# A gated-attention and mixture-of-experts kernel: expert 0's rest in 64-row pairs, with turns on VectorE

## The chip, the cores and the metric

One Trainium2 chip; the kernel runs on one core of it. The metric is the device time of one execution in microseconds (us), the median of the runs. TensorE (PE) multiplies, VectorE (DVE), ScalarE (ACT) and GpSimd (POOL) work element by element, SyncE (SP) and POOL issue the DMAs.

## The reference

```python
# attention: q, k, v, o_gate (4, 8, 768, 40); a state C, n, m per batch and head
for t in range(S):
    m_new = np.maximum(f_gate[:, :, t] + m, i_gate[:, :, t])
    f_stab = np.exp(f_gate[:, :, t] + m - m_new)
    i_stab = np.exp(i_gate[:, :, t] - m_new)
    C = f_stab * C + i_stab * einsum('bhd,bhe->bhde', vt, kt)
    n = f_stab * n + i_stab * kt
    y[:, :, t] = sigmoid(o_gate) * (C @ qt) / max(abs(n . qt), 1)
x = y.transpose(0, 2, 1, 3).reshape(3072, 320)
# experts: w1 (8, 320, 1024), w2 (8, 1024, 320)
logits = x @ w_gate + log1p(exp(x @ w_noise)) * noise
top2, top2_w = the two largest of 8 and their softmax
for e in range(8):
    out[tokens of e] += weight * (np.maximum(x[tokens of e] @ w1[e], 0) @ w2[e])
```

## The kernel before

**Stages.** The attention runs in 24 units of 128 tokens. Its rows go to DRAM (`rows`), and the gate, the choice of two experts and each token's rank within its expert are worked out beside it, in steps of a generator (`g_part`) that VectorE does in between. After the attention the eight experts follow one another. For each, POOL gathers the token rows into `XG`, tile by tile (128 rows, 7 tiles at most); the rows are turned so that the 320 features lie on partitions; the first product (`mm1` or `mm1_rows`) gives `hx`, 1024 by tokens; ScalarE evicts its relu (`HH`), VectorE the low part (`HLO`); the second product (`mm2`) gives y for 128 tokens, VectorE scales it, and POOL adds it into the output rows by an indirect DMA (`put`). Every operand is split into a high and a low part and a product is three: high by high, low by high, high by low. ScalarE makes the high part, VectorE the low one.

**Experts 0 and 1** have their tokens in two pieces, the first 384 columns and a rest of 416 (`E0S`), since the first piece is known earlier. The order is: first piece of 0 (`mm1(0, 0, f)`, eight passes `f`), its outputs (`first_outputs(0)`), first piece of 1, its outputs, rest of 1 (`mm1(1, 1, f)`), its four tiles of outputs (`mm2(1, t)`, t = 3 to 6), rest of 0, its outputs, and then experts 2 to 7 whole. `first_outputs` holds three sums in PSUM and goes through them three times, 72 products; its `events` are steps of other work that are put between two products. One of them is `advance`, which counts a unit up, does a share of the routing on VectorE, and sends the products for ranks (`ranks`, lines 480 to 482) and for the one-hot bursts (line 491) to PE once their unit has come (`lag`).

**Turning.** Experts 0 and 1 turn their rows on PE (`transpose_x`, line 883), ScalarE and VectorE writing the halves `XH` and `XL` from PSUM. With three blocks of 128 features a pass of `mm1` has 8 products: 128 rows of weights twice and 64 rows once, the last with two parts side by side. Experts 2 to 7 turn on VectorE in blocks of 32 (`turn_x`, to `XB`), 16 DMAs bring the blocks to their places (`spread_x`, to `XT`), ScalarE and VectorE split them (`split_x`, to `XH5`, `XL5`), and `mm1_rows` takes five blocks of 64 features, two products at a time on the two halves of the array's rows, each half for other rows of `hx` (`j` and `j + 4`).

**Queues.** The code is written in the order in which each engine does its work. Each engine takes its instructions in order, so an instruction that waits holds all behind it on its engine; SP and POOL do so with the DMAs that they issue. The PSUM banks of the experts have names: `s0` and `s1` with two buffers each, `e`, `xt`, `st`, `o`. `bank("h")` goes round `s0`, `s1`, `e` for `mm1`, `bank("x")` gives those of the transposes, `bank("y")` those of `mm2`.

Of the kernel before, what the change touches and what calls it, by code (L numbers as in the profile page):

```python
# [51 lines left out]
TURNS2 = {3: (3, 4), 4: (5,), 5: (6,)}  # L52
REST = (3, 4, 5, 6)
SPLITS2 = (5, 0, 3, 2)
# [20 lines left out]
def build(ctx, tc, qk, vk, og, fi, noise, wgn, w1, w2, cst, ce, out):  # L75
# [980 lines left out]

    def split_x(e):
        QC, QO = quarters(e)
        for h in range(2):
            c = slice(QO[2 * h], QO[2 * h] + 2 * QC[2 * h])  # L1060
            fx = lambda a: a[:, c].rearrange("p (q t c) -> p q t c", q=2, c=32)
            fh = lambda a: a[:, c].rearrange("p (t q c) -> p q t c", q=2, c=32)
            for k in range(5):
                A.activation(fh(XH5[:, k]), fx(XT[:, k]), AF.Copy)  # L1064
                V.tensor_sub(fh(XL5[:, k]), fx(XT[:, k]), fh(XH5[:, k]).bitcast(F32))  # L1065
                yield
# [77 lines left out]
    def mm2(e, t, between={}, base=None):  # L1144
# [3 lines left out]
        if t < 6:  # L1148
            c = slice(128 * t, 128 * t + n)
            for j in range(8):  # L1150
                T.matmul(ps[0:n], HH[:, j, c], W2H[:, j], start=j == 0, stop=False)  # L1151
                T.matmul(ps[0:n], HH[:, j, c], W2L[:, j], start=False, stop=False)  # L1152
                T.matmul(ps[0:n], HLO[:, j, c], W2H[:, j], start=False, stop=j == 7)  # L1153
                if j in between:
                    between[j]()
        else:

            for j in range(8):
                T.matmul(ps[0:2 * n], HT[:, j, 0:2 * n], W2H[:, j], start=j == 0, stop=False)
                T.matmul(ps[0:2 * n], HT[:, j, 0:2 * n], W2L[:, j], start=False, stop=j == 7)  # L1160
            A.activation(y[0:n], ps[n:2 * n], AF.Copy)
            V.tensor_add(y[0:n], y[0:n], ps[0:n])
            ps = y
# [57 lines left out]
    side = split_w1(staged, V)  # L1221
    def first_outputs(e, events):
        sums = [bank("h")[:, 0:DM] for _ in range(3)]
# [40 lines left out]
    lag[:] = 14, 14  # L1264
    rest = iter(range(7 - 1, 8))
    turn_ = iter(range(3))
    for t, y in first_outputs(0, at((lambda: transpose_x(next(turn_)), (3, 8, 13)), (lambda: next(side), (18, 40, 48)),
# [6 lines left out]
    load_w1(0, RAW1)  # L1274
# [13 lines left out]
    turn_ = iter(REST)  # L1288
    for t, y in first_outputs(1, at((low_w2b, range(2, 34, 4)), (lambda: advance(0.3), range(1, 40, 2)),
                                    (lambda: transpose_x(next(turn_)), (46, 52, 58, 64)))):  # L1290
        put(1, t, y)
# [4 lines left out]
    turns = lambda *ts: {n: (lambda t=t: transpose_x(t)) for n, t in zip((2, 4, 6), ts)}  # L1296
    weigh(1, 1)
    load_w2(0)
    gather(0, 1)
    side = split_w1(RAW1, V)  # L1300
    for f in range(8):
        mm1(1, 1, f)
        next(dealing, None)
        if f > 3:
            next(side)
    run(dealing)
    gather(2, ts=(0, 1, 2))
    for n, t in enumerate(REST):
        y = mm2(1, t, turns(*((3, 4, 5), (6,), (), ())[n]))
        next(side, None)  # L1310
        put(1, t, y)
        if not n:
            weigh(0, 1)
        if n == 1:
            gather(2, ts=(3, 4))
        if n == 2:
            gather(2, ts=(5, 6))
        if n < 3:
            turn_x(2, n)
    rows_w1(2)  # L1320
    side = split_w2()
    for f in range(8):
        mm1(0, 1, f)
        next(side)
        for t in TURNS2.get(f, ()):
            turn_x(2, t)
        if f == max(TURNS2):
            spread_x(2)
            weigh(2)
# [9 lines left out]
    XH5 = m2.tile([128, 5, NT], FR, name="xh5")  # L1339
# [217 lines left out]
```

## Time and profile before

| | |
|---|---|
| runs | 505.16, 502.9, 505.0 us; median 505.0 |
| profiled execution | 501.79 us, of which the span is 500.0; mean granted clock 0.992 |
| PE busy | 482.9 us, 97% of the span, 5653 matmuls |
| VectorE, ScalarE, POOL busy | 331.7 (66%), 249.3 (50%), 230.9 (46%) |
| read and written in HBM | 53.51 and 17.28 MB, 142 GB/s over the span |

The profile is one execution; times in it count from the start of the span. A row of the timeline gives the start, the time in us, the engine, the line of the code, the operation with its tile, and in brackets how long the engine had been idle and what ended that. PE's starts are measured and its ends modelled, so two products overlap in the rows; PE's pace is read from one start to the next. In the table by stage the first number is the length of the stretch, and then each engine's busy time in it with its count of instructions. DMA times to landing count from the issue.

### The profile page before, as it was taken

The page shows a single profiled execution, that of the slowest core. Times are in us where ns is not written, and L with a number is a line of the kernel's source. Part 1 is how long each engine was busy: PE and PEld are TensorE (multiplying, and loading weights), DVE is VectorE, ACT ScalarE, POOL GpSimd, SP SyncE. Part 2 cuts the span into 40 slices and gives each one's busy share as a digit, 9 for nine tenths or more (in the row PEclk, how much of TensorE's full clock was granted, in tenths as well). Part 3 has the DMA queues.
Part 4 walks back from the last instruction along what each step waited for, and adds up shares of the span by engine and source line. Part 5 has one row for each costly group of instructions (what it writes and reads, how often), then busy time and mean ns, then how long its engine had stood idle before and what let it go on. Part 6 is the DMA issues. An engine that isn't in the chain of part 4 may idle for free.

```text
span 500.0 us, 14344 instructions
## 1 busy us (share of the span) xinstructions
PE 482.9 (97%) x5653; PEld 451.1 (90%) x5653; DVE 331.7 (66%) x899; ACT 249.3 (50%) x604; POOL 230.9 (46%) x302
## 2 busy tenths in 40 slices
PE   8899999998999999999999999999999999999995
PEld 4677778777998999999999999999999999999994
DVE  7888988987599657585774566285637548554410
ACT  7687887798645244354551444063424605513400
POOL 9656675275404374828138306801850480142043
PEclk9899998999999999999999999999999999999999
DMA  6899787887799562859579528926971891682032
GB/s 166 229 262 269 218 242 202 230 225 214 232 384 279 138 120 54 184 112 263 137 149 267 135 53 209 248 41 139 254 139 42 206 256 26 141 176 37 4 39 41
DMA packets 62025, 84.52 MB, mean 169 GB/s; under 512 B 10790, under 2 KB 50347, under 8 KB 61920
## 3 DMA queue, kind: packets, MB, share of 16 engines
q1 hardware_dynamic: 49584, 59.21, 44.5%
q0 software_dynamic: 12368, 24.33, 23.0%
q8 instruction: 46, 0.75, 0.6%
q14 instruction: 27, 0.22, 0.1%
HBM read 53.51 MB, written 17.28 MB: 142 GB/s over the span
## 4 chain that ended last, share of the span: by engine, by line
PE 85%; DVE 6%; POOL 2%; ACT 2%; DMA 2%; issue 2%; SPq 0%; POOLq 0%; ACTq 0%; DVEq 0%
PE s L1091 17%; PE e L1091 8%; PE s L1105 6%; PE o L1151 5%; PE o L1153 5%; PE o L1152 5%; PE st L1151 5%; PE st L1153 4%; PE st L1152 4%; PE o L404 3%; PE s L365 3%; PE e L1105 3%; PE st L394 2%; PE e L342 2%; PE xt L427 2%
## 5 line engine op out<-in xcount | busy, mean ns | idle before, releaser
L1177 POOL DMA_INDIRECT y_out<-y,tok x53 | 86.3, 1628 | 167.3 <-DVE y L1167 150.6
L1129 ACT ACTIVATE hx<-s 128x384 fp32r<-128x384 f32 (+3 forms) x85 | 39.3, 496 | 71.8 <-PE s L1091 57.0
L1132 DVE SCALAR_TENSOR_TENSOR hx<-s,hx 128x384 fp32r<-128x384 f32 (+1 forms) x85 | 44.8, 548 | 37.5 <-ACT hx L1129 37.2
L854 POOL DMA_INDIRECT xg<-rows,tok x53 | 57.7, 1088 | 22.3 <-issue 13.1
L1151 PE MATMUL o<-w2h,hx 128*128 128x320 f32 (+1 forms) x184 | 57.3, 311 | 0.0
L1153 PE MATMUL o<-w2h,hx 128*128 128x320 f32 (+1 forms) x184 | 56.7, 308 | 0.0
L1152 PE MATMUL o<-w2l,hx 128*128 128x320 f32 (+1 forms) x184 | 56.6, 308 | 0.0
L1151 PE MATMUL st<-w2h,hx 128*128 128x320 f32 x152 | 47.5, 312 | 0.0
L1153 PE MATMUL st<-w2h,hx 128*128 128x320 f32 x152 | 46.9, 308 | 0.0
L1152 PE MATMUL st<-w2l,hx 128*128 128x320 f32 x152 | 46.8, 308 | 0.0
L1064 ACT ACTIVATE xh<-xt__124 128x384 fp32r<-128x384 f32 (+1 forms) x60 | 27.1, 528 | 20.2 <-DMA xt__124<-xb 16.5
L416 POOL TENSOR_TENSOR raw<-tm,vk 128x320 f32<-128x320 f32 x24 | 21.1, 877 | 31.7 <-ACT vk L351 11.3
L351 ACT ACTIVATE vk<-vk 128x320 f32<-128x320 f32 x72 | 33.8, 469 | 2.8 <-DMA vk<-og_in 1.9
L1151 PEld LDWEIGHTS o<-w2h,hx 128*128 128x128 f32 (+1 forms) x184 | 34.4, 187 | 0.5 <-issue 0.5
L1152 PEld LDWEIGHTS o<-w2l,hx 128*128 128x128 f32 (+1 forms) x184 | 34.5, 187 | 0.0
L1153 PEld LDWEIGHTS o<-w2h,hx 128*128 128x128 f32 (+1 forms) x184 | 34.3, 187 | 0.0
L1091 PE MATMUL s<-xh,w1h 64*128 64x384 f32 (+3 forms) x320 | 34.1, 340 | 0.0
L1091 PE MATMUL s<-xl,w1h 64*128 64x384 f32 (+3 forms) x320 | 34.0, 338 | 0.0
L1091 PE MATMUL s<-xh,w1l 64*128 64x384 f32 (+3 forms) x320 | 33.7, 337 | 0.0
L365 PEld LDWEIGHTS s<-qk 64*64 64x64 f32 x768 | 26.0, 141 | 8.5 <-issue 6.5
L1167 DVE TENSOR_SCALAR y<-o,gw 128x320 f32<-128x320 f32 x22 | 12.1, 551 | 32.4 <-PE o L1153 32.4
L1065 DVE TENSOR_TENSOR xl<-xt__124,xh 128x384 fp32r<-128x384 f32 (+1 forms) x60 | 31.2, 568 | 2.7 <-ACT xh L1064 1.9
(321 smaller groups left out, 1327.0 us busy)
## 6 DMA issues: line engine op xcount, KB each, us to landing
raw<-w_in SPq DMA_DIRECT2D x14, 640.0 KB, 12.7
raw<-w_in SPq DMA_DIRECT2D x7, 1280.0 KB, 10.3
xt__124<-xb SPq DMA_DIRECT2D x72, 120.0 KB, 3.2
qk<-qk_in SPq DMA_DIRECT2D x24, 256.0 KB, 4.6
y_out<-zrow SPq DMA_DIRECT2D x15, 320.0 KB, 7.0
vk<-vk_in POOLq DMA_DIRECT2D x24, 162.0 KB, 4.7
vk<-vk_in SPq DMA_DIRECT2D x24, 162.0 KB, 5.4
vk<-og_in SPq DMA_DIRECT2D x24, 160.0 KB, 4.3
```

The costliest lines, as they stand in the source:

```text
L351: A.activation(g, g, (AF.Exp, AF.Ln, AF.Exp)[p], bias=float(p == 1), scale=(-1.0, 1.0, -1.0)[p])
L365: T.matmul(SQ[u][:, p][half[p], h, :], q[r, 1, h, :], q[r, 0, h, :], start=True, stop=True)
L854: P.indirect_dma_start(out=XG[0:rows_of(e, t), t], out_offset=None, in_=XD[0:n], in_offset=bass.IndirectOffsetOnAxis(ap=token(e, t), axis= ...
L1065: V.tensor_sub(fh(XL5[:, k]), fx(XT[:, k]), fh(XH5[:, k]).bitcast(F32))
L1091: T.matmul(ps[y][:, 0:n], a[r, k, s], x[r, k, c], start=i == 0, stop=i == len(ops) - 1)
L1105: T.matmul(ps[:, 0:n], l, r, start=i == 0, stop=i == len(ops) - 1)
L1129: A.activation(hi, x, AF.Relu)
L1132: V.scalar_tensor_tensor(lo, top[0], 0.0, top[1].bitcast(F32), op0=OP.max, op1=OP.subtract)
L1151: T.matmul(ps[0:n], HH[:, j, c], W2H[:, j], start=j == 0, stop=False)
L1152: T.matmul(ps[0:n], HH[:, j, c], W2L[:, j], start=False, stop=False)
L1153: T.matmul(ps[0:n], HLO[:, j, c], W2H[:, j], start=False, stop=j == 7)
L1177: apart(e, P.indirect_dma_start(out=out, out_offset=bass.IndirectOffsetOnAxis(ap=token(e, t), axis=0), in_=y[0:n], in_offset=None, **(how ...
```

## The change

It turns expert 0's rest on VectorE and multiplies it with `mm1_rows`, as experts 2 to 7. For that its gathers are issued one by one, each behind expert 1's transpose of the same tile of `XG` (`turn_and_gather`), ahead of the puts of expert 1's first outputs; the turns stand behind passes 1 and 2 of `mm1(1, 1, f)` (`TURNS0`); `spread_rest` brings 96 columns a quarter (128 in the first) to `XT` in 16 DMAs; `rows_w1(0)` loads the first weights in blocks of 64 rows; and `split_rows_w1` and `split_rest` stand between the tiles of `mm2(1, t)` (`SPLITS1`). `first_outputs` names its banks itself, its transposes too, and `lag` for the ranks is 18 in place of 14 there. `mm2` of expert 0 takes the column blocks in the order `JS`. `weigh(1, 1)` moves ahead of expert 1's transposes.

```diff
--- before.py
+++ after.py
@@ -49,8 +49,12 @@
 GATES = (6, 4, 4, 4, 4, 4, 4)
 LEAD = 2
 TURNS = {0: (0,), 1: (1,), 2: (2,), 3: (3,), 4: (4, 5), 5: (6,)}
-TURNS2 = {3: (3, 4), 4: (5,), 5: (6,)}
+TURNS0 = {1:(3,4),2:(5,6)}
+TURNS1 = {1:(0,1,2)}
+TURNS2 = {0: (3, 4), 1: (5, 6)}
 REST = (3, 4, 5, 6)
+JS = (0, 1, 2, 4, 5, 6, 3, 7)
+SPLITS1 = (3,2,0,5)
 SPLITS2 = (5, 0, 3, 2)
 SPLITS = (2, 2, 3, 3, 3, 2, 0)
 OR1 = (0, 6, 1, 2, 3, 4, 5)
@@ -1054,6 +1058,25 @@
             for m in range(4):
                 SP.dma_start(XT[32 * m:32 * m + 32, :, c], XB[r, 5 * (m % 2):5 * (m % 2) + 5, 0:QC[q]])
 
+    def spread_rest():
+        for q in range(4):
+            r = slice(32 * q, 32 * q + 32)
+            n = 96 if q else 128
+            for m in range(4):
+                SP.dma_start(XT[32 * m:32 * m + 32, :, 128 * q:128 * q + n], XB[r, 5 * (m % 2):5 * (m % 2) + 5, 96:96 + n])
+
+    def split_rest():
+        c, d = E0S[1], E0S[1] + 384
+        for k in range(5):
+            x = XT[:, k, 0:512].rearrange("p (q t c) -> p q t c", q=4, c=32)[:, :, 0:3]
+            to = lambda a: a[:, k, c:d].rearrange("p (t q c) -> p q t c", q=4, c=32)
+            A.activation(to(XH5), x, AF.Copy)
+            V.tensor_sub(to(XL5), x, to(XH5).bitcast(F32))
+            if k == 4:
+                A.activation(XH5[:, :, d:NS], XT[:, :, 96:128], AF.Copy)
+                V.tensor_sub(XL5[:, :, d:NS], XT[:, :, 96:128], XH5[:, :, d:NS].bitcast(F32))
+            yield
+
     def split_x(e):
         QC, QO = quarters(e)
         for h in range(2):
@@ -1141,18 +1164,16 @@
         else:
             later.append(rest)
 
-    def mm2(e, t, between={}, base=None):
+    def mm2(e, t, base=None):
         n = rows_of(e, t)
         ps = bank("y")[:, 0:DM]
         y = m2.tile([128, DM], F32, name="y", bufs=TA + 1)
         if t < 6:
             c = slice(128 * t, 128 * t + n)
-            for j in range(8):
+            for j in (JS if e == 0 else range(8)):
                 T.matmul(ps[0:n], HH[:, j, c], W2H[:, j], start=j == 0, stop=False)
                 T.matmul(ps[0:n], HH[:, j, c], W2L[:, j], start=False, stop=False)
                 T.matmul(ps[0:n], HLO[:, j, c], W2H[:, j], start=False, stop=j == 7)
-                if j in between:
-                    between[j]()
         else:
 
             for j in range(8):
@@ -1219,8 +1240,12 @@
 
     wipe = lambda: next(clear, None)
     side = split_w1(staged, V)
+    def open_bank(name):
+        return psum.tile([128, 512], F32, name=name, bufs=2 if name in ("s0", "s1") else 1)
+
     def first_outputs(e, events):
-        sums = [bank("h")[:, 0:DM] for _ in range(3)]
+        sums = [open_bank(name)[:, 0:DM] for name in (("s0","s1","s0"),("s0","s1","e"))[e]]
+        turn["h"] += 2
         for k, (l, r) in enumerate(((HH, W2H), (HLO, W2H), (HH, W2L))):
             for n in range(24):
                 t, j = divmod(n, 8)
@@ -1261,17 +1286,18 @@
             next(side)
         advance(0.7 if f < 4 else 0.3, 4, True)
     weigh(1, 0)
-    lag[:] = 14, 14
+    lag[:] = 18,14
     rest = iter(range(7 - 1, 8))
     turn_ = iter(range(3))
-    for t, y in first_outputs(0, at((lambda: transpose_x(next(turn_)), (3, 8, 13)), (lambda: next(side), (18, 40, 48)),
+    free = iter(("xt","st","s1"))
+    for t, y in first_outputs(0, at((lambda: transpose_x(next(turn_), open_bank(next(free))), (3, 8, 14)), (lambda: next(side), (18, 40, 48)),
                                     (lambda: low_w2(next(rest)), (2,6)),
                                     (wipe, range(1, 72, 2)), (lambda: advance(0.2), range(1, 36, 2)),
                                     (lambda: advance(0.3), range(37, 72, 2)))):
         held[t] = y
     for _ in clear:
         pass
-    load_w1(0, RAW1)
+    rows_w1(0)
     lag[:] = 6,4
     for f in range(8):
         mm1(1, 0, f, later)
@@ -1286,45 +1312,51 @@
         V.tensor_sub(W2L[:, x], RAW2[:, x], W2H[:, x].bitcast(F32))
 
     turn_ = iter(REST)
+
+    def turn_and_gather():
+        x = next(turn_)
+        transpose_x(x)
+        gather(0, ts=(x,))
+
     for t, y in first_outputs(1, at((low_w2b, range(2, 34, 4)), (lambda: advance(0.3), range(1, 40, 2)),
-                                    (lambda: transpose_x(next(turn_)), (46, 52, 58, 64)))):
-        put(1, t, y)
+                                    (lambda: weigh(1, 1), (44,)), (turn_and_gather, (46, 52, 58, 64)))):
+        held[t] = y
+    for t in range(3):
+        put(1, t, held[t])
     assert done[0] == NU
     while routing:
         fill(1.0)
     dealing = deal()
-    turns = lambda *ts: {n: (lambda t=t: transpose_x(t)) for n, t in zip((2, 4, 6), ts)}
-    weigh(1, 1)
     load_w2(0)
-    gather(0, 1)
-    side = split_w1(RAW1, V)
     for f in range(8):
         mm1(1, 1, f)
         next(dealing, None)
-        if f > 3:
-            next(side)
+        for t in TURNS0.get(f, ()):
+            turn_x(0, t)
+        if f == max(TURNS0):
+            spread_rest()
     run(dealing)
+    weigh(0, 1)
     gather(2, ts=(0, 1, 2))
+    XH5 = m2.tile([128, 5, NT], FR, name="xh5")
+    side = chain(split_rows_w1(), split_rest())
     for n, t in enumerate(REST):
-        y = mm2(1, t, turns(*((3, 4, 5), (6,), (), ())[n]))
-        next(side, None)
-        put(1, t, y)
-        if not n:
-            weigh(0, 1)
-        if n == 1:
-            gather(2, ts=(3, 4))
-        if n == 2:
-            gather(2, ts=(5, 6))
-        if n < 3:
-            turn_x(2, n)
+        for _ in range(SPLITS1[n]):
+            next(side, None)
+        put(1, t, mm2(1, t))
+        if n in (1, 2):
+            gather(2, ts=(2 * n + 1, 2 * n + 2))
+        for x in TURNS1.get(n, ()):
+            turn_x(2, x)
     rows_w1(2)
     side = split_w2()
-    for f in range(8):
-        mm1(0, 1, f)
+    for j in range(4):
+        mm1_rows(0, 1, j)
         next(side)
-        for t in TURNS2.get(f, ()):
+        next(side)
+        for t in TURNS2.get(j, ()):
             turn_x(2, t)
-        if f == max(TURNS2):
+        if j == max(TURNS2):
             spread_x(2)
             weigh(2)
     V.tensor_copy(toki, cs[:, C_TOK:C_TOK + NU])
@@ -1336,7 +1368,6 @@
     P.tensor_add(ov, ov, rf)
     P.tensor_scalar(ov, ov, float(BLK), None, op0=OP.is_ge)
     P.tensor_mul(OVM[:, :, 2:4], WTS[:, :, 0:2], ov)
-    XH5 = m2.tile([128, 5, NT], FR, name="xh5")
     side = chain(split_rows_w1(), split_x(2))
     for n, t in enumerate(REST):
         for _ in range(SPLITS2[n]):
```

PE, end of expert 0's first outputs (tile `e` or `s_2898` is the third sum; L480 to L482 are the ranks; L1105 or L1128 is the first pass of expert 1). Before:

```order
L1227 MATMUL s_2897<-w2l,hx 128x320 x8
L1227 MATMUL e<-w2l,hx 128x320 x2
L480 LDWEIGHTS tri
L480 MATMUL st<-xt__124,tri 128x64
L481 LDWEIGHTS ones
L481 MATMUL st<-xt__124,ones 128x64
L482 LDWEIGHTS ones
L482 MATMUL st<-xt__124,ones 128x8
L1227 MATMUL e<-w2l,hx 128x320 x6
L1105 MATMUL s_3063<-xl,w1h 128x384 x5
```

and of the change:

```order
L1252 MATMUL s_2897<-w2l,hx 128x320 x8
L1252 MATMUL s_2898<-w2l,hx 128x320 x8
L1128 MATMUL e<-xl,w1h 128x384 x5
L1128 MATMUL e<-xl,w1l 128x384 x3
L484 LDWEIGHTS tri
L484 MATMUL st<-xt__124,tri 128x64
L485 LDWEIGHTS ones
L485 MATMUL st<-xt__124,ones 128x64
L486 LDWEIGHTS ones
L486 MATMUL st<-xt__124,ones 128x8
L1128 MATMUL s_3070<-xl,w1h 128x384 x5
```

The ranks moved from the middle of the third sum to behind expert 1's first pass, and that pass begins on `e`.

VectorE, expert 1's four tiles of second products (`y<-o`, `y<-st` scale a tile; `xl` is the low part of x, `w1l` that of expert 0's first weights, `xb` a turn). Before:

```order
L886 TENSOR_TENSOR xl<-xt,xl 128x2x128
L887 TENSOR_TENSOR xl<-xt,xl 64x128
L1167 TENSOR_SCALAR y<-o,gw 128x320
L172 TENSOR_TENSOR w1l<-raw_119,w1h 128x512
L846 TENSOR_TENSOR gw_2710<-xg,km 128x8
L847 TENSOR_TENSOR gw<-gw_2710 128x4
L1048 STREAM_TRANSPOSE xb<-xg 128x5x2x32
L886 TENSOR_TENSOR xl<-s_3555,xl 128x2x32
L887 TENSOR_TENSOR xl<-s_3555,xl 64x32
L1167 TENSOR_SCALAR y<-st,gw 128x320
```

and of the change:

```order
L850 TENSOR_TENSOR gw_2710<-xg,km 128x8
L851 TENSOR_TENSOR gw<-gw_2710 128x4
L1099 TENSOR_TENSOR w1l<-raw_119,w1h 128x512 x3
L1188 TENSOR_SCALAR y<-o,gw 128x320
L1099 TENSOR_TENSOR w1l<-raw_119,w1h 128x512 x2
L1188 TENSOR_SCALAR y<-st,gw 128x320
L1052 STREAM_TRANSPOSE xb<-xg 128x5x2x32 x3
L1188 TENSOR_SCALAR y<-o,gw 128x320
L1074 TENSOR_TENSOR xl<-xt__124,xh_3502 128x4x3x32 x5
L1077 TENSOR_TENSOR xl<-xt__124,xh_3502 128x5x32
L1183 TENSOR_TENSOR y<-y,st 32x320
```

The low parts of x left the first tiles and stand behind the scaling of the third, tile 5.

SP, from expert 0's second weights (L832 or L836) to expert 2's first (L1071 or L1094). Before:

```order
L832 DMA raw_123<-w_in 128x8x320
L824 TENSOR_LOAD who
L1071 ISA
L1071 DMA raw_119<-w_in 64x5x512
L1071 ISA
L1071 DMA raw_119<-w_in 64x5x512
```

and of the change:

```order
L836 DMA raw_123<-w_in 128x8x320
L1066 DMA xt__124<-xb 32x5x128 x4
L1066 DMA xt__124<-xb 32x5x96 x12
L828 TENSOR_LOAD who
L1094 ISA
L1094 DMA raw_119<-w_in 64x5x512
```

Sixteen DMAs of the spread came in between.

## Rows read from the trace of the kernel before

**Rows 1.** Page, part 4: who held the chain that ended last, by engine
```profile
PE 85%; DVE 6%; POOL 2%; ACT 2%; DMA 2%; issue 2%; SPq 0%; POOLq 0%; ACTq 0%; DVEq 0%
```

**Rows 2.** Table by stage: core 0; columns us, PE, PEld, DVE, ACT, POOL busy, PEclk, DMA share, GB/s
```profile
140.40:154.34 13.94, 12.63 (x93) 11.88 (x93) 13.49 (x60) 5.55 (x14) 0.50 (x2) 1.00 1.03 377
...
178.56:190.51 11.95, 11.95 (x66) 11.95 (x65) 7.30 (x24) 5.71 (x11) 7.05 (x7) 1.00 0.54 86
190.51:204.91 14.40, 14.40 (x102) 13.97 (x101) 9.17 (x25) 3.80 (x8) 9.36 (x10) 1.00 0.53 128
204.91:216.86 11.95, 11.95 (x66) 11.95 (x65) 9.15 (x27) 6.58 (x15) 7.16 (x12) 1.00 0.44 94
216.86:229.84 12.98, 12.98 (x90) 12.57 (x90) 9.12 (x20) 5.93 (x12) 6.18 (x6) 1.00 0.88 189
```

**Rows 3.** Timeline, PE, first outputs of expert 0: start, us, engine, line, op, idle before
```profile
143.36 0.54 PE L1227 MATMUL s<-w2h,hx 128*128 128x320 f32 x2
144.45 1.45 PE L1227 MATMUL e<-w2h,hx 128*128 128x320 f32 x8 [0.55 <-DVE hx L1132]
```

**Rows 4.** Timeline, PE, their end and the first pass of expert 1
```profile
151.91 0.46 PE L1227 MATMUL e<-w2l,hx 128*128 128x320 f32 x2
152.96 0.21 PE L480 MATMUL st<-xt__124,tri 128*128 128x64 bf16 x1 [0.60 <-DVE xt__124 L639]
...
153.38 1.12 PE L1227 MATMUL e<-w2l,hx 128*128 128x320 f32 x6
...
155.74 1.04 PE L1105 MATMUL s<-xl,w1h 128*128 128x384 f32 x5
```

**Rows 5.** Timeline, ScalarE and VectorE, around the rank products
```profile
153.36 0.93 ACT L1232 ACTIVATE y<-s,gw 128x320 f32<-128x320 f32 x2
...
155.12 0.19 DVE L661 TENSOR_TENSOR xt__124<-xt__124,bump 128x16 f32<-128x16 f32 x1
...
157.91 0.68 DVE L702 TENSOR_TENSOR xt__124<-spot,xt__124 128x1024 f16<-128x1024 f16 x1
```

**Rows 6.** Timeline, PE, expert 3's pairs of 416 columns
```profile
279.29 1.11 PE L1091 MATMUL s<-xh,w1h 64*128 64x416 f32 x10
...
284.96 0.35 PE L1091 MATMUL e<-xh,w1h 64*128 64x416 f32 x1
```

**Rows 7.** Timeline, PE, end of expert 0 and first pairs of expert 2
```profile
229.60 0.30 PE L1160 MATMUL st<-w2l,hx 128*64 128x320 f32 x1
229.84 1.28 PE L1091 MATMUL s<-xh,w1h 64*128 64x448 f32 x10
```

**Rows 8.** Timeline, POOL and PE, gathers and first transpose for expert 1's rest
```profile
166.82 1.00 POOL L854 DMA_INDIRECT xg<-rows,tok  x1 [0.30 <-issue]
168.12 1.12 POOL L854 DMA_INDIRECT xg<-rows,tok  x1 [0.31 <-issue]
...
173.42 0.49 PE L883 MATMUL xt<-cs,xg 128*128 128x128 f32 x3
```

**Rows 9.** By line: gathers (L854, 160 to 262); spread (L1055), whole, then its first sixteen
```profile
DMA to landing us min/median/max: 2.2/3.2/9.4
...
L1055 SPq DMA_DIRECT2D xt__124<-xb x96: 585/610/1858, 216.3 to 436.7; - x96
...
DMA to landing us min/median/max: 2.3/3.2/5.4
...
216.35 11.86 SPq L1055 DMA_DIRECT2D xt__124<-xb  x16
```

**Rows 10.** Timeline, VectorE and ScalarE: eviction, turns, splits of x
```profile
180.80 0.56 DVE L1132 SCALAR_TENSOR_TENSOR hx<-e,hx 128x384 fp32r<-128x384 f32 x1 [2.07 <-ACT hx L1129]
...
212.69 0.89 DVE L1048 STREAM_TRANSPOSE xb<-xg 128x320 f32<-128x320 f32 x2
...
224.81 2.45 ACT L1064 ACTIVATE xh<-xt__124 128x448 fp32r<-128x448 f32 x5 [4.23 <-DMA xt__124<-xb]
...
235.02 1.02 DVE L1065 TENSOR_TENSOR xl<-xt__124,xh 128x384 fp32r<-128x384 f32 x2
```

## The prediction

> **What bounds the kernel now.** First the chain of waits: TensorE (PE) is 85% of what ended last [rows 1]. So time is won only where PE works less or stands still less, and it counts in full only where PE has no slack. The table by stage says where that holds [rows 2]: of the stages that the change touches PE is busy for all of each but the first, expert 0's first outputs, with 12.63 of 13.94 us. Expert 0's second products, the last stage shown, are full too (12.98 of 12.98), so what is won ahead of expert 2 is carried on.
>
> Where PE stood is read from the timeline by start-to-start distances, since its ends are modelled. The last stage holds 3 x 24 + 16 = 88 products of 320 columns and one change of the array's shape at its end (0.10, part 5): 12.88 / 88 = 0.146 a product. In expert 0's first outputs two products begin at 143.36, so the next was due at 143.65; it began at 144.45, waiting for VectorE's L1132 on bank `e`: 0.80 [rows 3]. Later two begin at 151.91, the next was due at 152.20 and began at 153.38, behind three rank products that waited for VectorE's L639: 1.18 [rows 4].
>
> **The change part by part,** in us, against the profiled execution (501.79, span 500.0), which stands 3.2 below the median of the runs shown (505.0). I take the same difference off both.
>
> 1. *Banks of the first outputs.* Three sums go to `s0`, `s1`, `s0`, so none waits for the last eviction from `e`; the transposes go to banks that are long free. Gain 0.80.
>
> 2. *Ranks later* (lag 18). The three products move behind the first pass of expert 1. A pass is 1.40 (154.34, where the first stage ends, to 155.74 [rows 4]). PE comes 1.98 earlier to that pass and is through it near 153.8; VectorE's order up to the scan is the same and the ranks had their scan before 153.38, so the wait goes. The products keep an estimated 0.09. Gain 1.09. What is late next: the one-hot steps. On ScalarE the rank copy now stands behind a third scaling of y, an eviction and a part of W2: from 153.36 on [rows 5] three scalings at 0.47, the eviction and the W2 part at some 0.4 and the copy at 0.2 end near 155.7, so VectorE's chain starts there where it started at 155.12, and one more eviction (0.5) stands in it. The burst's last step began at 157.91 and took 0.68 [rows 5]; it now ends 0.6 + 0.5 later, near 159.7. PE is there after five passes, at 159.45: minus 0.25. Together 1.64; bounds 0.8 (the gain of the ranks all lost) and 1.9.
>
> 3. *No transposes for expert 0's rest.* Expert 1's second products are 88 as well and take 14.40 with the twelve transposes [rows 2]; without them 12.88. They go: 1.52.
>
> 4. *64-row pairs.* Before, 8 x 8 products of 416 columns take 11.95 [rows 2]. After, 4 x 15 pairs. Expert 3's pairs of 416 columns show the price: from 279.29 to 284.96 there are six rows of five pairs each, 5.67 for 30, 0.189 a pair [rows 6]. 60 x 0.189 = 11.34: 0.61 won.
>
> 5. *Two more changes of the array's shape,* full rows to halves and back. At expert 2 the first pair begins 0.24 after the last full product (229.60 to 229.84 [rows 7]) instead of 0.146. I take 0.10 for each way: minus 0.20. The Trainium skill, TensorEngine Tiling (Array Packing), Key Properties, says that changing the tiling mode drains TensorE, which speaks against putting halves between two full-row stages; it gives no figure. Were a drain as long as a whole modelled product (0.30 in rows 7), two would cost 0.6 and the sum be 3.0; the trace agrees that there is a gap, and shows it smaller.
>
> 6. *Early turns, spread and splits.* Added: four turns on VectorE (0.89 for two [rows 10]), 16 DMAs on SP, 6 splits of x and 5 of W1 for 6 of W1 before, on ScalarE and VectorE. They cost nothing while the columns come in time. Expert 1's rest begins at 178.56 - 1.64 = 176.9. Each gather is issued after its tile's transpose (the first 173.42 before, 171.8 now); four at 1.30 apart on POOL start from 172.2 to 176.1 [rows 8] and land a median 3.2 later [rows 9]: 179.3. VectorE turns tiles 3 and 4 behind the second eviction and 5 and 6 behind the third. A pass is 11.95 / 8 = 1.49, and the first eviction started at 180.80 [rows 10], 0.75 after its pass; with two turns ahead the third starts near 182.6 and the last turn ends near 184.0. The evictions run up to 1 us late for that, which the five `h` buffers cover. Then SP: 16 issues at a median 0.61 take 9.8, the landing 3.2 more [rows 9]: XT full at 197.0. The slow end is the 11.86 that expert 2's sixteen took, with the longest landing, 5.4 [rows 9]: 201.3. ScalarE then needs 2.45 for five splits [rows 10] and 0.35 for the tail: 199.8. PE wants them at 176.9 + 11.95 + 12.88 = 201.8. So there is 2.0 of cover, and XT later than 199.0 costs one for one. VectorE's low parts wait for the scaling of tile 5, PE's end of which is 2.34 before 201.8; with 0.75 as above and 5 x 0.51 (two in 1.02 [rows 10]) + 0.25 they are done at 203.0, and wanted after five pairs, at 202.85. I take 0.15 for that; bounds of the whole part 0 and 2.3.
>
> 7. *Puts behind the second gathers on POOL:* nobody waits before the y buffers come round, in expert 1's second products. *weigh early:* on VectorE it waits for expert 1's four gathers, the last at 168.12 [rows 8], some 0.7 later now, landed near 172; behind it stand the transposes' low parts, wanted at 176.9. *Columns 3 and 7 last* (`JS`): keeps PE off the last eviction. All at nothing, covered by PE's work.
>
> Sum: 1.64 + 1.52 + 0.61 - 0.20 - 0.15 = **3.4 faster**: 498.4 for a profiled execution, 505.0 - 3.4 = **501.6** as median. With punctual columns the bounds give 4.0 at best (1.9 + 1.52 + 0.6) and 2.3 at worst (0.8 + 1.52 + 0.6 - 0.6).
>
> **The rivals.**
> *B, the routing keeps the pace.* The removed rank wait comes back whole at the bursts. For: in the first stage VectorE is busy 13.49 of 13.94 [rows 2], and the 0.25 of part 2 is already such a wait. Against: the chain to the bursts is only one eviction longer. Gain 0.8 in place of 1.64: 2.6 in all, or 502.4.
>
> *C, late columns.* The spread runs at the slow rows, XT is full at 201.3, PE stalls 2.3 and the gain is 1.1: 503.9. For: expert 2's sixteen did take 11.86. Against: the DMA engines' share was 0.88 in their stage, and is 0.54 and 0.53 in the two where the new ones run [rows 2]. The Trainium skill, DMA: Bandwidth & Descriptors, Specifications, asks for at least 512 B a transfer for line rate and says that below it SDMA does read-modify-write; twelve of the new DMAs move pieces of 384 B. By that rule the spread is slow and this case holds; no row of before shows such a piece on this path.
>
> *D, slower.* VectorE, in order, stops at the turn of tile 6 because its gather lands 9.4 after its start, the longest in rows 9: 185.5. The turn ends at 186.1, the slow spread at 203.4, the splits at 206.2, 4.4 behind PE: 1.0 slower, 506.0. It decides from XT at 202.4 on. For: the gathers now run beside the load of expert 0's second weights. Against: the median landing is 3.2.
>
> *E, the halves don't run side by side.* Then 120 products take some 22 and the kernel loses 8. The pairs of expert 3 have the same layout and 0.189 a pair [rows 6], so this is all but excluded.
>
> **How the numbers follow.** Forecast A 0.57, B 0.15, C 0.14, D 0.06, E 0.01, and 0.07 for something on neither list that leaves no visible change. A alone reaches from 501.0 to 502.7. To hold 8 in 10 the range takes in A, B and C, with half of a 0.5% error of measurement at either end of the likely ones: 500.0 to 504.4. A measurement of this kernel tells about 0.5% (2.5) from no change. Faster by more: nine tenths of A and half of B, 0.58. Slower by more: the late end of D (XT after 204.9) and E, 0.05. The rest, 0.37, lies within.
>
> **What the profile after would show.** Right: no wait of PE for L1132 and L639 in the first outputs; expert 1's second products in 12.9 and without a TensorE transpose; expert 0's rest in 11.3 to 11.6, its pairs at equal starts; expert 2 beginning 3.4 earlier, near 226.4, and that distance kept to the end. B shows as idle time of PE before the bursts, C and D as idle time at the first or sixth pair of expert 0's rest, put down to ScalarE or VectorE, whose own wait is the DMA from `xb`. Wrong would be a start of expert 2 after 228.5, or a gain there that is gone at the end.

## The result, and the profile after

The changed kernel takes **498.75 us** (median of 17 executions, 496.21 to 504.89) against 504.7 for the kernel before beside it (17, 499.55 to 507.32): ratio 0.9905, 95% interval 0.9879 to 0.9930. The ratio leaves out the executions that stand over 1.5% above the fastest of their kernel, so it is not the quotient of the two medians. The forecast was 501.6, within 500.0 to 504.4. It is faster, as forecast, and the median lies 1.25 below the range. Against the median of the runs shown the kernel gained 6.2 where 3.4 was forecast; by the ratio, 4.8. Two later comparisons give 0.9946 and 0.9947, that is 2.7. So the first question is which of these the change is worth.

The profiled execution took 497.22 us. From its page, the head and the chain that ended last, by engine:

```profile
span 495.4 us, 14440 instructions
PE 479.3 (97%) x5696; PEld 448.2 (90%) x5697; DVE 331.1 (67%) x900; ACT 248.2 (50%) x605; POOL 232.3 (47%) x302
PE 82%; DVE 6%; POOL 3%; SPq 2%; DMA 2%; issue 2%; ACT 1%; POOLq 0%; DVEq 0%; ACTq 0%
```

The table by stage, in the same stages as [rows 2]: expert 0's first outputs, expert 1's rest, its second products, expert 0's rest, its second products.

```profile
139.63:151.49 11.86, 11.86 (x90) 11.74 (x90) 11.51 (x53) 3.44 (x9) 0.00 (x0) 1.00 1.06 380
176.06:188.02 11.96, 11.96 (x66) 11.95 (x65) 7.14 (x25) 4.16 (x8) 5.69 (x7) 1.00 0.55 88
188.02:200.99 12.97, 12.97 (x89) 12.57 (x88) 8.79 (x22) 5.53 (x12) 9.58 (x9) 1.00 0.70 166
200.99:212.56 11.57, 11.57 (x121) 11.06 (x120) 8.73 (x27) 5.36 (x13) 7.79 (x14) 1.00 0.57 133
212.56:225.69 13.13, 13.13 (x90) 12.59 (x89) 10.18 (x24) 6.69 (x14) 5.63 (x5) 1.00 0.91 195
```

The first stage fell from 13.94 to 11.86 and PE is busy in all of it. Expert 1's second products fell from 14.40 to 12.97, expert 0's rest from 11.95 to 11.57. The timeline of PE shows where the waits of [rows 3, 4] were, then the two places where the array's shape changes:

```profile
147.89 3.77 PE L1252 MATMUL s<-w2l,hx 128*128 128x320 f32 x24
151.49 1.05 PE L1128 MATMUL e<-xl,w1h 128*128 128x384 f32 x5
...
152.91 0.21 PE L484 MATMUL st<-xt__124,tri 128*128 128x64 bf16 x1
...
153.20 1.15 PE L1128 MATMUL s<-xl,w1h 128*128 128x384 f32 x5
...
200.76 0.30 PE L1181 MATMUL st<-w2l,hx 128*64 128x320 f32 x1
200.99 1.22 PE L1114 MATMUL s<-xh,w1h 64*128 64x416 f32 x10
202.05 1.12 PE L1114 MATMUL s<-xl,w1h 64*128 64x416 f32 x10
...
203.96 1.11 PE L1114 MATMUL s<-xh,w1h 64*128 64x416 f32 x10
204.91 1.11 PE L1114 MATMUL s<-xl,w1h 64*128 64x416 f32 x10
...
225.46 0.30 PE L1181 MATMUL st<-w2l,hx 128*64 128x320 f32 x1
225.69 1.29 PE L1114 MATMUL s<-xh,w1h 64*128 64x448 f32 x10
```

Twenty-four products stand in one row with no wait in them (151.49 - 147.89 = 3.60, 0.150 each), and the ranks (L484) stand behind the first pass. The late columns, in the timelines of SP, ScalarE and VectorE:

```profile
183.94 10.38 SPq L1066 DMA_DIRECT2D xt__124<-xb  x16
...
197.32 2.19 ACT L1073 ACTIVATE xh<-xt__124 128x384 fp32r<-128x384 f32 x5 [5.98 <-DVE xb L1052]
199.41 0.32 ACT L1076 ACTIVATE xh<-xt__124 128x160 fp32r<-128x160 f32 x1
...
201.59 0.32 DVE L1077 TENSOR_TENSOR xl<-xt__124,xh 128x160 fp32r<-128x160 f32 x1
```

For ScalarE's start at 197.32 the profile names VectorE's L1052, a turn of expert 2; the columns themselves were there before it, since by the trace's records of the DMA packets the last one of the spread ended at 196.36. ScalarE was done at 199.73, PE's first pair came at 200.99: 1.26 of cover. The low parts were ready at 201.91; the sixth pair came at 202.05, 0.1 later than five pairs at their pace of 0.189 would have it. Whether the low parts or the change of shape made that 0.1 is not to be seen here.

From the start of expert 0's first outputs to expert 2's first pair PE took 229.84 - 140.40 = **89.44** before and 225.69 - 139.63 = **86.06** after: 3.38 less. Behind that point the two kernels are the same (270.2 and 269.7 to the span's end). This distance, called *the changed stretch* below, is what the experiments compare.

### The profile page after: what moved, and what is told of

Same layout as the page of the kernel before. It is cut to its first block, busy times and chain, and to the rows that moved or that the text cites. A ratio compares the mean times of both kernels' runs of the same rounds, so it can differ in the third digit from the quotient of the medians.

```text
span 495.4 us, 14440 instructions
## 1 busy us (share of the span) xinstructions
PE 479.3 (97%) x5696; PEld 448.2 (90%) x5697; DVE 331.1 (67%) x900; ACT 248.2 (50%) x605; POOL 232.3 (47%) x302
## 4 chain that ended last, share of the span: by engine, by line
PE 82%; DVE 6%; POOL 3%; SPq 2%; DMA 2%; issue 2%; ACT 1%; POOLq 0%; DVEq 0%; ACTq 0%
PE s L1114 19%; PE e L1114 8%; PE o L1174 6%; PE o L1175 5%; PE o L1176 5%; PE s L1128 5%; PE st L1174 5%; PE st L1175 4%; PE st L1176 4%; PE s L1252 4%; PE o L408 3%; PE e L1128 2%; PE s L369 2%; DVE p L383 2%; PE st L398 1%
## 5 line engine op out<-in xcount | busy, mean ns | idle before, releaser
L1114 PE MATMUL s<-xh,w1h 64*128 64x384 f32 (+3 forms) x350 | 37.6, 341 | 0.0
L1114 PE MATMUL s<-xl,w1h 64*128 64x384 f32 (+3 forms) x350 | 37.3, 339 | 0.0
L1114 PE MATMUL s<-xh,w1l 64*128 64x384 f32 (+3 forms) x350 | 37.0, 337 | 0.0
L1114 PEld LDWEIGHTS s<-xh,w1h 64*128 64x128 f32 x350 | 31.2, 185 | 1.2 <-issue 1.1
```

Of the source, the lines that this page charges most:

```text
L1114: T.matmul(ps[y][:, 0:n], a[r, k, s], x[r, k, c], start=i == 0, stop=i == len(ops) - 1)
```

## The experiments

Two theories. *First:* the change is worth its sum, 3.4, all in the changed stretch, and what the medians show beyond it is the spread of the executions. *Second:* something else in the program is faster too.

**The changed kernel again** (no edit).

> The change once more, unedited. Theory 1 (the parts sum as predicted, and what the first comparison showed beyond that is scatter of the attention stage): from the first product of expert 0's first outputs to expert 2's first pair the trace takes 86.0 us where before took 89.4, and the time comes out 3.4 to 3.8 us under before, ratio 0.992 to 0.9935. Theory 2 (over 1 us is won systematically somewhere that the prediction did not look, in the attention or behind expert 2): ratio 0.989 to 0.991 again, with the first pass of expert 0 again near 126.4 or earlier, where before has 127.2.

Ratio 0.9946 (0.9912 to 0.9980). The changed stretch is 85.89, 3.55 less than before; but its span is 503.2, since expert 0's first pass (the same code in both kernels) began at 133.96 in place of 126.45. PE's waits up to that point, of this kernel in two executions, first the one above, then this one (columns: us in total, times, longest):

```profile
PE st L398 <- issue: 1.9, 2, 1.4
PE s L369 <- DMA qk<-qk_in: 1.8, 2, 1.4
...
PE e L346 <- DMA re<-hl: 1.1, 2, 0.8
...
PE s L369 <- issue: 0.6, 1, 0.6
```

```profile
PE e L346 <- DMA re<-hl: 2.9, 5, 0.8
PE st L398 <- issue: 2.6, 2, 1.5
PE s L369 <- DMA qk<-qk_in: 2.5, 3, 1.6
PE s L369 <- issue: 2.1, 3, 1.3
PE xt L431 <- issue: 1.9, 1, 1.9
```

All rows of that view add up to 9.7 and 16.6: the same program waited 6.9 longer in its attention stage, for its DMAs and for "issue". So one profiled span does not tell 3 us.

**The first outputs alone**: banks and lag of the change in the kernel before. **The rest alone**: the changed kernel with banks and lag of before.

```diff
...
-        sums = [bank("h")[:, 0:DM] for _ in range(3)]
+        sums = [open_bank(name)[:, 0:DM] for name in (("s0","s1","s0"),("s0","s1","e"))[e]]
+        turn["h"] += 2
...
-    lag[:] = 14, 14
+    lag[:] = 18,14
...
-    for t, y in first_outputs(0, at((lambda: transpose_x(next(turn_)), (3, 8, 13)), (lambda: next(side), (18, 40, 48)),
+    for t, y in first_outputs(0, at((lambda: transpose_x(next(turn_), open_bank(next(free))), (3, 8, 14)), (lambda: next(side), (18, 40, 48)),
```

> Before, with only the banks of the first outputs and the lag of 18. Theory 1: the first outputs of expert 0 fall from 13.94 to 11.9 us, the next eight passes grow by 0.3, everything behind keeps its length; 1.7 us faster, ratio 0.9965. Theory 2 if the surplus hangs on this part: 2.7 or more, ratio 0.9945 or less. Rival B of the prediction (the routing keeps the pace): the next eight passes grow by 1 us, 0.8 faster.

> The change, with the first outputs' banks, transposes and lag as before. Theory 1: the two waits of 0.80 and 1.18 are back, expert 1's second products take 13.0 and expert 0's rest 11.6; 1.7 to 1.9 us faster than before, ratio 0.9965. Theory 2 if the surplus hangs on this part: 3 us, ratio 0.994.

First outputs alone: changed stretch 87.74 (1.70 less than before), ratio 0.9945 (0.9909 to 0.9981). Rest alone: 87.68 (1.76 less), ratio 0.9987 (0.9953 to 1.0021). The two add up to 3.46, the whole within 0.1, so neither needs the other. The two ratios, for gains equal to 0.06 in the trace, lie 0.4% apart.

**Splits earlier**: `SPLITS1 = (3,2,5,0)` and block 3 sixth in `JS`, so that the low parts are never late.

> The change, with the splits of x one tile earlier (SPLITS1 = 3, 2, 5, 0) and expert 0's column blocks in the order 0, 1, 2, 4, 5, 3, 6, 7. Theory 1: the 0.1 us before the sixth pair of expert 0's rest and the 0.13 us in the middle of its first tile of second products go; 0.2 to 0.3 us under the change. Rival: the columns are not all there at 196, VectorE waits for them ahead of the scaling of tile 5 and the last put is later; PE does not see it, same time.

Expert 0's rest took 11.56 in place of 11.57, its second products 13.25 in place of 13.13; ratio 0.9933 (0.9898 to 0.9969). The expectation was wrong, and it tells where the 0.1 comes from: VectorE's low parts were now done 1.4 before the first pair, and the sixth pair still came 1.06 after it, as in the profile after. From the timelines of VectorE and PE:

```profile
199.38 0.32 DVE L1077 TENSOR_TENSOR xl<-xt__124,xh 128x160 fp32r<-128x160 f32 x1
...
201.13 1.22 PE L1114 MATMUL s<-xh,w1h 64*128 64x416 f32 x10
202.19 1.11 PE L1114 MATMUL s<-xl,w1h 64*128 64x416 f32 x10
```

So the low parts were never late; the 0.1 belongs to the change of the array's shape, as a second part behind the first pair. The trace of the kernel before has it too, where expert 2 begins at 229.84: the first five pairs take 1.12, the next five 1.01 (timeline of PE).

```profile
230.96 1.17 PE L1091 MATMUL s<-xl,w1h 64*128 64x448 f32 x10
231.97 1.19 PE L1091 MATMUL s<-xh,w1l 64*128 64x448 f32 x10
```

From here on a run is a single execution unless a ratio is given with it, so stretches are compared and not times.

**Banks alone**: the diff above without its `lag` line, in the kernel before. **Lag alone**: that line only.

> The kernel before with the change's banks for the first outputs and its places for the transposes there, and nothing else (the ranks keep lag 14). First theory (the terms of the prediction stand on their own): expert 0's first outputs lose the 0.80 for the bank, so PE reaches the rank products 0.80 earlier, where VectorE has its step no sooner: the wait of 0.60 there grows to about 1.2 to 1.4 unless VectorE's chain comes earlier by as much. The stretch then takes between 13.1 (gain kept) and 13.9 (gain lost at the ranks). If it keeps the gain, the two parts add up as the sum has them; if it loses it, the banks are worth nothing without the lag, and the 1.7 belongs to both together. Second theory (the gain at the banks is only contention that goes with any reordering): no definite place, a stretch of 13.9 with a wait on the bank left.

> The kernel before with lag 18 for the ranks and nothing else. First theory: the wait on the bank stays (0.80), the rank products leave the stretch with their wait of 1.09 and their own 0.09, which takes 12.75 in place of 13.94; the first pass stage of expert 1 takes 12.05 to 12.4 in place of 11.96, since the rank products stand in it and the bursts may be waited for. Net from the start of expert 0's first outputs to expert 1's second ones 0.8 to 1.1 less. Second theory (the routing on VectorE sets the pace, so the wait comes back at the bursts): the stretch of expert 1's passes grows by over 0.8 and nothing is won.

With the banks alone PE comes to the ranks 0.80 earlier and waits 0.80 longer: the first stage stays at 13.95. VectorE's L639, which the ranks wait for, comes no sooner, 12.21 after the start of the stage in both kernels (152.61 - 140.40 and 153.05 - 140.84; timeline of VectorE, kernel before, then banks alone):

```profile
152.61 0.32 DVE L639 COPY xt__124<-base 128x8 bf16<-128x8 bf16 x1
...
153.05 0.32 DVE L639 COPY xt__124<-base 128x8 bf16<-128x8 bf16 x1
```

Then expert 1's passes take 13.41 in place of 11.96. The table by stage shows why: the granted clock (third from the right) is 0.51, the lower of its two levels (1.2 GHz), for 3.4 us.

```profile
140.84:154.79 13.95, 12.38 (x93) 11.90 (x93) 13.49 (x60) 5.56 (x14) 0.50 (x2) 1.00 1.03 374
154.79:158.20 3.41, 3.41 (x13) 3.41 (x12) 3.01 (x11) 1.29 (x4) 0.73 (x1) 0.51 0.78 158
```

With the lag alone the wait for the bank is there (0.56) and the one for the ranks is not: 12.68 and 12.07, together 1.15 less than before (table by stage):

```profile
139.13:151.81 12.68, 12.12 (x90) 11.75 (x90) 12.26 (x56) 4.26 (x11) 0.00 (x0) 1.00 1.06 386
151.81:163.88 12.07, 12.07 (x85) 11.58 (x84) 11.15 (x42) 7.68 (x19) 5.67 (x7) 1.00 0.89 212
```

So the gains do not belong to the edits as the prediction has them.

**The banks once more**, and **the banks with lag 16**, which puts four products more ahead of the ranks.

> The kernel of the run with the banks alone, unchanged. There PE waited 1.42 for VectorE at the rank products, and right behind it the granted clock was 0.50 for some 3.5 us, so the first pass stage of expert 1 took 13.41 in place of 11.96. First theory (a wait of that length brings the clock down each time): the wait is 1.2 to 1.5 again, the clock falls again, and the stage takes 13.2 to 13.6. Second theory (the fall was chance and has nothing to do with the wait): the same wait, no fall, and 11.95 to 12.4.

> The banks with lag 16: four of the six products that stood behind the ranks now stand ahead of them (4 x 0.146 = 0.58), so PE waits 0.58 less there (0.85 in place of 1.42) and expert 0's first outputs take 13.95 - 0.58 = 13.36. First theory (the clock falls behind a wait of 1.42 and not behind a shorter one, as before with its 0.60): no fall, and the first pass stage of expert 1 takes 11.95 to 12.3; from the start of the first outputs to expert 1's second ones 25.4, so the banks now keep some 0.5. Second theory (the clock falls behind this wait too): 13.2 to 13.6 for that stage and 26.8 in all, worse than the kernel before (25.90).

The timeline of PE at the ranks, of the banks once more, then with lag 16:

```profile
157.99 0.21 PE L480 MATMUL st<-xt__124,tri 128*128 128x64 bf16 x1 [1.43 <-ACT w1h L171]
...
159.38 1.04 PE L1105 MATMUL e<-xl,w1h 128*128 128x384 f32 x5
160.25 0.69 PE L1105 MATMUL e<-xl,w1l 128*128 128x384 f32 x3
```

```profile
155.91 0.21 PE L480 MATMUL st<-xt__124,tri 128*128 128x64 bf16 x1 [0.84 <-ACT w1h L171]
...
156.71 1.04 PE L1105 MATMUL e<-xl,w1h 128*128 128x384 f32 x5
```

The rows name ScalarE's L171 for the end of the wait; the weight load of the same product waited 1.7 for VectorE's L639, which ended at 157.95, 0.04 ahead of the product. It is the same wait of 1.43, and this time no fall: 13.96 and 11.88, together 25.84 against 25.90 before. With lag 16 the wait is 0.84 and the two stages take 25.28. So the banks alone are worth nothing. Behind a wait of 1.4 the clock fell in one run of two, at a cost of 13.41 - 11.88 = 1.5; none of the other fourteen traces has a fall at this place. PE's 0.80 at the bank and 1.09 at the ranks hung on one chain of VectorE: whatever brings PE to the ranks earlier only waits there until they are moved.

**The spread twice**: `spread_rest()` is called twice, so the columns come later.

> The changed kernel with the sixteen DMAs of expert 0's spread issued twice, the second time with the same data, so that the last columns come some 10.4 us later (the length of the sixteen issues in the profile after). First theory (the cover of the late columns is short and real, and beyond it lateness costs one for one): ScalarE's last part of the split was done at 199.73 and PE's first pair began at 200.99, 1.26 later; so PE stalls 10.4 - 1.3 = 9.1 at the first pair, put down to ScalarE, whose own wait is the DMA from xb; the stall is kept to the end, 9 us in the stretch from expert 0's first outputs to expert 2's first pair (86.0 becomes 95). Second theory (that lateness is paid back, because expert 2's gathers, spread and weights run on during the stall): expert 2 begins 9 later but ends earlier by a part of that, over 0.5. Third (two spreads overlap in the queues, so the second costs little): a stall under 5.

PE waited 9.71 for ScalarE's L1076 (9.1 was expected), and behind that the pairs ran at the lower level for 5.9 us:

```profile
215.13:221.00 5.87, 5.87 (x34) 5.66 (x36) 1.53 (x5) 0.62 (x2) 3.18 (x8) 0.50 0.72 133
221.00:229.32 8.32, 8.32 (x90) 8.03 (x86) 7.81 (x24) 4.71 (x12) 0.00 (x0) 1.00 0.09 19
```

Expert 0's rest took 14.19 in place of 11.57. The changed stretch is 98.57, 12.5 longer; expectation 95. From expert 2's first pair to the end it is 269.8, as ever: nothing is paid back.

**Five more spread DMAs**, the case of late columns at about the size that the prediction gave it.

```diff
-    def spread_rest():
-        for q in range(4):
+    def spread_rest(more=0):
+        for i in [*range(16), *range(more)]:
+            q, m = divmod(i, 4)
...
-            spread_rest()
+            spread_rest(5)
```

> The changed kernel with the first five of expert 0's sixteen spread DMAs issued again behind them, with the same data: 5 x 0.70 = 3.5 us later, less the cover of 1.26, so PE stalls 2.2 to 2.4 at the first pair of expert 0's rest, as in the prediction's case of late columns. First theory (lateness costs one for one, as the prediction has it): expert 1's second products and expert 0's rest together take 24.54 + 2.3 = 26.8, and from expert 0's first outputs to expert 2's first pair 88.4, still 1.0 less than before. Second theory (a stall of that length brings the clock down, and the pairs behind it run slowly for a while): expert 0's rest takes 12.9 to 14.2 in place of 11.57, the two together 28 to 29.5, and nothing of the gain is left (89.7 to 91 against 89.44 before).

The timeline of PE at the first pair, then the table by stage:

```profile
199.25 0.30 PE L1181 MATMUL st<-w2l,hx 128*64 128x320 f32 x1
202.92 1.21 PE L1114 MATMUL s<-xh,w1h 64*128 64x416 f32 x10 [3.37 <-ACT xh L1076]
```

```profile
202.92:204.00 1.08, 1.08 (x12) 1.07 (x14) 1.08 (x4) 0.41 (x1) 0.78 (x2) 1.00 1.05 210
204.00:207.00 3.00, 3.00 (x22) 2.87 (x20) 0.45 (x2) 0.00 (x0) 2.61 (x6) 0.55 1.04 211
```

The stall was 3.4, one more than expected, and the clock fell behind it: expert 1's second products and expert 0's rest took 16.41 + 13.13 = 29.54 in place of 24.54, the changed stretch 91.09 in place of 86.06. That is 1.65 *more* than the kernel before. One for one falls as a price; the second theory of this run holds. In the six traces that have this rest and no such stall the clock did not fall in these stages.

**The plain order of column blocks** in expert 0's second products: `JS = (0, 1, 2, 3, 4, 5, 6, 7)`.

> The changed kernel with expert 0's second products in the plain order of column blocks, 0 to 7. First theory (the order was worth nothing): block 3 is wanted for its low part by the twelfth product, 11 x 0.146 = 1.6 after the first (at 214.17 in the profile after), where VectorE had it at 214.05; so no wait or one under 0.2, and expert 0's second products take 12.95 to 13.2, as after (13.13 and 12.96). Second theory (the order keeps PE off the last eviction, as the prediction says): without it a wait of 0.4 to 1.0 at the first tile, and 13.4 to 14.0.

They took 13.25 with no wait at block 3 or 7; the changed stretch is 86.17. The order is worth nothing that shows. In the traces with the change's rest these products took 12.96 to 13.25; what makes that difference was not settled.

**The kernel before once more**, **the change a third time**, and **the kernel before against itself**.

> The kernel before, unchanged, for a second trace of it. First theory (behind the attention everything repeats): the waits of 0.55 and 0.60 are there, no fall of the clock behind them, 13.9 and 12.0 for the two stages, 89.3 to 89.6 from expert 0's first outputs to expert 2's first pair, while the attention's end differs by up to some us. Second theory (the kernel before loses a fall of the clock at its rank wait in some executions, which the change then takes away): 13.2 to 13.6 for expert 1's first pass stage and 90.8 to 91.1 in all.

> The changed kernel, unchanged. First theory (worth 3.4 us, the rest is the spread of the attention stage): a ratio of 0.9932, within 0.990 to 0.9965, and in the trace 85.9 to 86.2 from expert 0's first outputs to expert 2's first pair. Second theory (worth 4.8 or more, something outside those stages is faster too): a ratio below 0.990.

> The kernel before, unchanged, against itself. First theory (the spread alone moves a median of a dozen executions by one to two us): a ratio of 0.997 to 1.003, not 1.000 exactly, with an interval some 0.006 to 0.008 wide, and single executions 6 to 9 us apart. Second theory (medians of such sets repeat to 0.1%, so the two ratios of the change mean two different gains): 0.999 to 1.001 with a narrow interval. In the trace 89.3 to 89.6 from expert 0's first outputs to expert 2's first pair.

| kernel | changed stretch | first pass of expert 0 begins | ratio to before (95%) |
|---|---|---|---|
| before, three traces | 89.44, 89.39, 89.42 | 127.22, 127.01, 124.70 | (itself) 0.9977 (0.9946 to 1.0007) |
| change, three traces | 86.06, 85.89, 86.13 | 126.45, 133.96, 132.73 | 0.9905 (0.9879 to 0.9930), 0.9946 (0.9912 to 0.9980), 0.9947 (0.9908 to 0.9987) |

The stretch repeats to 0.25 and differs by 89.42 - 86.03 = **3.39**. All that comes behind the attention repeats as well: from expert 0's first pass to the end of the span the kernel before takes 372.8, 372.5 and 372.6, the change 369.0, 369.2 and 369.5. In these traces the spread lies ahead of that pass. The kernel before against itself came out 1.5 us lower by its median (500.14 against 501.63), and its 12 executions lie 9.2 apart. So a median of a dozen executions moves by one or two us with nothing changed. 3.39 is a ratio of 0.9932 of 502: inside the second and third interval, just outside the first. The first comparison is off the others by about its own width; no trace shows a further gain behind it. Why the executions of the kernel before were slower in that first set (median 504.7, later 502.31 and 501.63) stays open, since none of them left a trace.

## Why the prediction was right or wrong

**What bounds it, and the sum: right.** PE's starts carried the whole gain, and nothing of it was given back by the end. 3.4 was forecast, 3.39 is there; a start of expert 2 3.4 earlier was named as the sign.

**Parts 1 and 2, banks and ranks: the sum right in part by luck, its terms wrong.** The two stages went from 25.90 to 24.15, 1.75 against 1.64. But 0.80 for the banks and 1.09 for the ranks do not stand by themselves: banks alone 0, lag alone 1.15, both 1.75. The wait that was feared at the bursts did not come, so case B falls. In its place the three rank products cost more than their 0.09: 0.29 from the first of them to the next pass (152.91 to 153.20), and the second stage is 0.33 longer than before (12.29 against 11.96) with no wait of PE in it. That is what the 0.09 and the 0.25 for the bursts come to.

**Parts 3 and 4: right.** Transposes with one change of shape: 14.40 - 12.97 = 1.43, against 1.52 - 0.10. The pairs kept 0.189 (from 203.96 to 204.91 is 0.95 for five).

**Part 5, changes of shape: too low by half.** The gap to the first pair is what [rows 7] showed, 0.23 at 200.76 and at 225.46, but five pairs behind it take 1.06 in place of 0.95. A change costs 0.08 + 0.11, some 0.2 in place of 0.10; [rows 7] shows only its first half; the second (1.12 against 1.01 for five pairs) stood right behind those rows in the same trace. The way back costs the same: 1.03 for the last five pairs, and 0.26 from the first full product to the second (211.53, 212.56, 212.82). Two changes come to 0.4, which stays below the 0.6 of two whole products.

**Part 6, late columns: the forecast right, the price wrong.** ScalarE began its splits 200.99 - 197.32 = 3.7 ahead of PE, where the prediction has XT full 201.8 - 197.0 = 4.8 ahead; the cover was 1.26 in place of 2.0. The 0.15 for the low parts was not needed, and balanced what part 5 lacked. The rule of the Trainium skill (DMA: Bandwidth & Descriptors, Specifications) on pieces below 512 B, on which case C leaned, did not bite: issues and landing took 10.38 and at most 3.0, to ScalarE's start, where 9.8 and 3.2 were forecast, and by the records of the trace after a packet of 384 B took 22 ns (median), one of 768 B in expert 2's spread 44. But "XT later than 199.0 costs one for one" fell: with a stall of 3.4 the clock fell, and 1.56 came on top (13.13 - 11.57). With a fall of that size case C, a gain of 1.1, becomes a loss of some 0.5, so the price of a late spread was set too low, and the slower side with it. The Trainium skill, TensorE: Matmul & The Clock Gate, What's actually happening, says that the default state of that clock "is throttled, and activity releases the throttle" and that the same kernel meets the gate in another phase from run to run; the pair of runs with the banks, one with a fall and one without behind the same wait, agrees.

**How the numbers follow: the step that failed.** The prediction took 3.4 off 505.0, the median of three runs, gave case A 501.0 to 502.7, and allowed half of 0.5%, that is 1.25, for the measurement. (From 501.0 that reaches down to 499.75; 500.0 was written.) The base was not known that well. The kernel before has medians of 504.7, 502.31 and 501.63 in the sets beside the change and 500.14 against itself, and single executions from 497.18 to 508.78. The median of all 87 of these executions is 502.24, and of all 41 of the changed kernel 499.11. 502.24 - 3.4 = 498.8 is what the first set of the change measured, 498.75. So the gain was sized right and the number that it was taken from was too high. A warning stood in the prediction itself: the profiled execution lay 3.2 below the median of the runs shown, and that difference was kept as if it were fixed; the sum from the profile, 498.4, is 0.35 off the measured median. A base that may lie two us to either side, which the range left out, makes of A 499.0 to 504.7, and 498.75 lies just under that edge. In the first comparison by itself the base was near 505.0 (504.7), so there the gain of 6.0 is larger than 3.39 by what no trace explains. Where single executions differ, the traces show, is ahead of expert 0's first pass; in the trace of before the DMA engines' share is 0.98 from 20 to 40 us and 0.86 from 40 to 60, and PE waits 1.7 for DMAs before that pass.

## What to carry to other kernels

Compare stretches of PE's starts across traces, and run the kernel before against itself, before a few us of a median are explained. Waits on one engine that hang on one chain of another are one term: cutting the first alone only lengthens the second. Price a stall of TensorE with the clock that may fall behind it, and keep cover for that.

## What the runs showed that was not expected

The clock also falls inside the attention. In the second trace of the kernel before it was at the lower level for most of this stretch, and not in the next (table by stage):

```profile
16.00:27.00 11.00, 9.02 (x143) 7.46 (x141) 6.39 (x15) 5.16 (x11) 4.89 (x12) 0.54 0.86 234
27.00:38.00 11.00, 10.27 (x256) 8.12 (x250) 8.64 (x19) 9.17 (x21) 5.53 (x10) 0.99 0.81 223
```

143 products in eleven us against 256. In other executions such falls begin near 52, 75, 100 or 117 us, or there are none. They are part of the spread and not all of it: of the four traces without one, three begin expert 0's first pass at 124.7, 124.8 and 126.0, but one at 130.8; those with one begin it from 126.45 to 133.96. And twice, in the runs with the banks once more and with lag 16, expert 2's first products took 26.15 and 24.26 in place of 22.91 at a clock of 1.00. PE's waits there are all for "issue" and come to 0.7 and 0.4; the rest of the 3.24 and 1.35 is products that start later than their pace with no wait shown. The DMA engines' share is 1.00 and 1.03 in the part that is long, and 1.06 in the same part of the kernel before, so it doesn't tell them apart. What held PE was not tried.
